# Two units of 768 columns in place of three of 512 for the rest tile of each batch

## The chip, the cores and the metric

One Trainium2 chip, one core. The metric is device time in microseconds (us) of the whole program. Runs agree within about 0.3%.

## The reference, cut to what matters

```python
# x: (4, 12416, 128), inducing: (32, 128); moe weights 128x1536, 128x1536, 1536x128
h = mab(inducing, x)                 # softmax attention, 32 rows a batch
y = mab(x, h)                        # softmax attention back to 12416 rows
out = (relu(y @ w_gate) * (y @ w_val)) @ w_out
```

12416 rows are 97 tiles of 128. The kernel works on pairs of 512-row blocks, eight tiles at once: 12 pairs make 96 tiles and one tile is left, the rest tile.

## The kernel before

The hidden width 1536 is twelve chunks of 128. A full unit is one chunk for a pair, 2 x 512 columns: gates into two PSUM banks (tag `g`, three banks in all), values into a two-bank buffer (tag `v`, two buffers), Relu of the gates on ScalarE, product on VectorE. Because `y @ w` is taken as `p2 @ (h @ w)`, a matmul contracts over only 32 rows, and matmuls on the four row groups of the array can overlap.

A rest unit is four chunks of one tile, 4 x 128 columns, all in one gate bank and one row group:

```python
for s in range(3):
    yield dict(
        mm=[[(slice(i * P, (i + 1) * P), 4 * s + i, p2[r : r + 32, 0:P], hgv[r : r + 32, :])
             for i in range(4)]
            for r in (0, 64)],              # r = 0: gates, r = 64: values
        dst=gvr[:, 4 * s : 4 * s + 4, :].rearrange("p i c -> p (i c)"))
```

The main loop walks in slots, one new unit in each. Here is its order (cut; a "fill" is a piece of other work):

```python
values()                       # TensorE: values of the unit of two slots ago
for m in unit["mm"][0]: gate(*m)   # TensorE: gates of the new unit
for f in post.pop(at, []): f()     # ScalarE etc.: copies of the slot before
# ... 1 to 3 steps of the output chain (o_ps, one bank), and at most one "fill"
nc.scalar.activation(..., func=AF.Relu)       # gates of the new unit
nc.vector.tensor_tensor(..., op=ALU.mult)     # product of the unit of two slots ago
```

A fill is a piece of other work. Three of them, near the end of each of the first three batches, are the pieces of `h @ w` for the next batch: four matmuls into a gate bank, and a 512-column copy on ScalarE one slot later.

```python
for k in range(3):
    ev_hgv(b, k, at + 2, at + 9 + 3 * k)      # earliest and latest slot
```

"The border" below is the passage from the last full units of a batch through its rest units to the first full units that follow.

The softmax here doesn't subtract the row's maximum and nothing guards it: scores larger than these inputs give would overflow.

Of the kernel before, what the change touches and what calls it, by code (L numbers as in the profile page):

```python
# [12 lines left out]
AF = mybir.ActivationFunctionType  # L13
# [5 lines left out]
def kernel(  # L19
# [20 lines left out]
    P = 128  # L40
# [23 lines left out]
    def st(shape, dtype, tag, bufs, name=None):  # L64
        return sb.tile(shape, dtype, tag=tag, bufs=bufs, name=name or tag)
# [273 lines left out]
    count = itertools.count()  # L339


    SPB = NPAIR * NFF + 3


    def slot(b, pr, s):
        if b == B - 1 and pr >= NPAIR - 1:
            return b * SPB + (NPAIR - 1) * NFF + (3 if pr < NPAIR else 0) + s
        return b * SPB + pr * NFF + s

    def order(b):  # L350
# [304 lines left out]
    def chain(w, gv, key, k, t0, first):  # L655
        c = {}
        nt = w // P

        def step(i):
            if i == 0:  # L660
                c["ps"] = bank("o", "o_ps")
            nc.tensor.matmul(  # L662
                c["ps"][:, 0:w], wo[:, i, :], gv(i), start=(i == 0), stop=(i == NFF - 1)
            )

        def evac(at):
            oT = st([P, BLK], FP16, "oT", 4)
            nc.scalar.copy(out=oT[:, 0:w], in_=c["ps"][:, 0:w])  # L668

            def tr():  # L670
                o16 = st([P, TPB, P], FP16, "o16", 4)
                nc.sync.dma_start_transpose(out=o16[:, 0:nt, :], in_=oT[:, 0:w])

                def scale():
                    osb = st([P, TPB, P], FP32, "osb", 4)
                    z = z2is[key + (k,)]
                    for t in range(nt):
                        zz = z[:, t, :]
                        nc.gpsimd.tensor_scalar(  # L679
                            out=osb[:, t, :],  # L680
                            in0=o16[:, t, :],
                            scalar1=zz,
                            scalar2=zz,
                            op0=ALU.mult,
                            op1=ALU.mult,
                        )

                    def store():
                        nc.sync.dma_start(
                            out=ov[key[0]][:, t0 : t0 + nt, :], in_=osb[:, 0:nt, :]  # L690
                        )

                    post[at + 8].append(store)

                post[at + 5].append(scale)

            post[at + 1].append(tr)

        if w == BLK:
            steps = [(first if i == 0 else 0, lambda i=i: step(i)) for i in range(NFF)]  # L700
            counts = (6, 5)
            if key[0] == B - 1 and key[1] == NPAIR - 2:
                counts = (6, 5) if k == 0 else (4, 4)
        else:
            steps = [(first + i // 4, lambda i=i: step(i)) for i in range(NFF)]
            counts = ([4, 8], [4, 8])
        job(steps, evac, counts)

# [69 lines left out]
    def units():  # L778
        for b in range(B):
            for pr in order(b):  # L780
                base = slot(b, pr, 0)
                p2, hgv = p2s.get((b, pr)), state[b]["hgv"]
                if (b, pr) == (B - 1, NPAIR - 1):
                    gvs = [st([P, 6, 2, BLK], FP16, "gv", 4) for _ in range(2)]
                    for k in range(2):
                        steps, evac = last_block(
                            lambda i, g=gvs[k]: g[:, i // 2, i % 2, :],
                            (b, pr),
                            k,
                            (2 * pr + k) * TPB,  # L790
                            k == 1,
                            lambda i, k=k: base + 3 + 6 * k + i // 2,
                        )
                        job(steps, evac, ([1, 3, 3, 3, 3] if k == 0 else [5] * 8,) * 2)
                    for u in range(NFF):
                        k = u // 6
                        p2 = p2s[(b, pr, k)]
                        yield dict(
                            mm=[
                                [  # L800
                                    (
                                        slice(d * BLK, (d + 1) * BLK),
                                        2 * (u % 6) + d,
                                        p2[r : r + 32, :],
                                        hgv[r : r + 32, :],
                                    )
                                    for d, r in ((0, 64 * j), (1, 64 * j + 32))
                                ]
                                for j in range(2)
                            ],  # L810
                            dst=gvs[k][:, u % 6, :, :].rearrange("p k c -> p (k c)"),
                            parts=2 if u == NFF - 1 else 1,
                        )
                elif pr < NPAIR:
                    gvs = []

                    def gv(i, k, gvs=gvs):
                        return gvs[i // 6][:, i % 6, k, :]

                    for k in range(2):  # L820
                        chain(
                            BLK,
                            lambda i, k=k, gv=gv: gv(i, k),
                            (b, pr),
                            k,
                            (2 * pr + k) * TPB,
                            base + 10 + 6 * k,
                        )
                    for s in range(NFF):
                        if s % 6 == 0:  # L830
                            gvs.append(st([P, 6, 2, BLK], FP16, "gv", 4))
                        yield dict(
                            mm=[
                                [
                                    (
                                        slice(k * BLK, (k + 1) * BLK),
                                        s,
                                        p2[r : r + 32, :],
                                        hgv[r : r + 32, :],
                                    )  # L840
                                    for k, r in ((0, 64 * j), (1, 64 * j + 32))
                                ]
                                for j in range(2)
                            ],
                            dst=gvs[-1][:, s % 6, :, :].rearrange("p k c -> p (k c)"),
                            parts=2 if base + s == 0 else 1,
                        )
                else:
                    gvr = st([P, NFF, P], FP16, "gvr", 1)
                    chain(P, lambda i, g=gvr: g[:, i, :], (b, pr), 0, NT - 1, base + 4)  # L850
                    for s in range(3):
                        yield dict(
                            mm=[
                                [
                                    (
                                        slice(i * P, (i + 1) * P),
                                        4 * s + i,
                                        p2[r : r + 32, 0:P],
                                        hgv[r : r + 32, :],
                                    )  # L860
                                    for i in range(4)
                                ]
                                for r in (0, 64)
                            ],
                            dst=gvr[:, 4 * s : 4 * s + 4, :].rearrange("p i c -> p (i c)"),
                        )

    def form(ps, cols, s, p2, hgv):
# [1 line left out]

    def gate_banks(unit):

        n = unit["dst"].shape[-1] // BLK
        unit["g"] = [None] * n

        def gate(cols, s, p2, hgv):
            k, lo = divmod(cols.start, BLK)
# [19 lines left out]
    while True:  # L897
# [64 lines left out]

        if unit:
            g16 = unit["g16"] = st([P, 2 * BLK], FP16, "g16", 4)
            for k, ps in enumerate(unit["g"]):
                nc.scalar.activation(out=g16[:, k * BLK : (k + 1) * BLK], in_=ps, func=AF.Relu)  # L966
        if ready:
            n = ready["dst"].shape[-1]
            w = n // ready.get("parts", 1)
            for a in range(0, n, w):  # L970
                nc.vector.tensor_tensor(  # L971
                    out=ready["dst"][:, a : a + w],
                    in0=ready["g16"][:, a : a + w],
                    in1=ready["v"][:, a : a + w],
                    op=ALU.mult,
                )
        at += 1

# [29 lines left out]
```

## Time and profile before

| what | before |
|---|---|
| time, median of 3 | 708.84 us |
| VectorE, ScalarE, TensorE busy | 96%, 96%, 90% |
| full products (128x1024) | 574, 1213 ns each, 654.9 us busy |
| rest products (128x512) | 12, 685 ns each, 8.0 us busy |
| VectorE idle in the second border of the trace (363.25 to 366.25) | 0.42 + 0.58 us |

VectorE and ScalarE are both nearly full, so the shares do not say which sets the pace. VectorE runs full products without a gap for 50 to 150 us at a time, and at each border it waits about 1 us for TensorE. ScalarE idles there too:

```profile
193.67 0.60 ACT L966 ACTIVATE g<-g_ps 128x512 f16<-128x512 f32 x1 [0.33 <-PE g_ps L869]
194.78 1.09 ACT L966 ACTIVATE g<-g_ps 128x512 f16<-128x512 f32 x2 [0.51 <-PE g_ps L869]
...
196.22 5.04 ACT L966 ACTIVATE g<-g_ps 128x512 f16<-128x512 f32 x10
```

These are ScalarE's lines of the first border: start, length, operation, count, and in brackets the idle time before with what ended it.

### The profile page before, as it was taken

To read this page: it belongs to the slowest core of one execution; us is meant where nothing else is said; L and a number is where in the kernel's file an instruction comes from. 1 tells how busy PE (TensorE), PEld (TensorE's weight loads), DVE (VectorE), ACT (ScalarE), POOL (GpSimd) and SP (SyncE) were. 2 spreads that over 40 slices of the span, in tenths; PEclk is the share of its full clock that TensorE was granted. 3 is DMA by queue.
4 is the path that set the end of the run, shared out by engine and by line. 5 is a ranking of instruction groups with operands and counts; after the bars stand their busy time and mean duration, and the time that the engine had idled before them with its cause. 6 is when DMAs were issued, how large, how long until landed. Compare 5 with 4: busy or idle time off the path is not lost. (4 is left out here: it accounts for less than half of the span.)

```text
span 706.6 us, 14082 instructions
## 1 busy us (share of the span) xinstructions
PE 637.6 (90%) x4629; PEld 186.5 (26%) x4629; DVE 677.7 (96%) x619; ACT 676.1 (96%) x1384; POOL 350.4 (50%) x646
## 2 busy tenths in 40 slices
PE   6899999999988999999998999999999888888997
PEld 5422222222222222222222222222222222222224
DVE  4699999999999999999999999999999999999997
ACT  5799999999999999999999999999999999999996
POOL 3627636544275637356255472753516443534543
PEclk9999999999999999999999999999999999999999
DMA  8656666431258867523149666653223132231222
GB/s 342 219 137 178 161 169 165 109 94 47 84 141 166 201 162 215 118 77 84 53 88 218 169 171 167 165 120 81 63 68 93 50 90 59 78 90 50 71 58 89
DMA packets 142346, 87.58 MB, mean 124 GB/s; under 512 B 117152, under 2 KB 125632, under 8 KB 139968
## 3 DMA queue, kind: packets, MB, share of 16 engines
q1 hardware_dynamic: 142128, 86.62, 46.6%
q8 instruction: 36, 0.59, 0.4%
q14 instruction: 38, 0.31, 0.2%
q10 hardware_dynamic: 144, 0.07, 0.0%
HBM read 27.80 MB, written 25.43 MB: 75 GB/s over the span
## 5 line engine op out<-in xcount | busy, mean ns | idle before, releaser
L971 DVE TENSOR_TENSOR gv<-g,v_ps 128x1024 f16<-128x1024 f16 (+1 forms) x578 | 657.5, 1209 | 9.9 <-PE g_ps L869 6.0
L966 ACT ACTIVATE g<-g_ps 128x512 f16<-128x512 f32 x1164 | 604.2, 618 | 11.9 <-PE g_ps L869 8.4
L662 PE MATMUL o_ps<-gv,wo 128*128 128x512 f16 x1128 | 352.6, 384 | 43.9 <-ACT oT L668 43.9
L679 POOL TENSOR_SCALAR osb<-o,z2i 128x128 f32<-128x128 f16 x380 | 165.9, 452 | 280.5 <-DMA o<-oT 278.6
L869 PE MATMUL g_ps<-p,hgv 32*128 32x512 f16 x1152 | 284.1, 380 | 1.7 <-ACT g L966 1.0
L869 PE MATMUL v_ps<-p,hgv 32*128 32x512 f16 x1152 | 223.6, 383 | 8.7 <-DVE gv L971 6.9
L869 PEld LDWEIGHTS <-hgv 32*128 32x128 f16 x2400 | 69.8, 91 | 267.2 <-issue 263.1
L662 PEld LDWEIGHTS <-wo 128*128 128x128 f16 x1176 | 81.0, 97 | 212.3 <-issue 195.9
L430 POOL TENSOR_TENSOR z2i<-zt,minus 128x16 f32<-128x16 f32 (+3 forms) x31 | 73.2, 2365 | 0.3
L668 ACT CAST oT<-o_ps 128x512 f16<-128x512 f32 (+1 forms) x98 | 58.4, 596 | 0.1
L501 POOL CAST x<-x 128x2048 f16<-128x2048 f32 x18 | 34.0, 1890 | 14.1 <-DMA x<-in_x_dram 13.9
L423 POOL TENSOR_TENSOR zt<-zt 128x32 f32<-128x32 f32 (+5 forms) x124 | 35.1, 283 | 9.7
L423 POOL TENSOR_TENSOR zt<-p2T 128x256 f32<-128x256 f16 (+3 forms) x31 | 17.4, 562 | 24.3 <-DMA p2T<-p 14.0
L270 DVE COPY xT<-xT_ps 128x1024 f16<-128x1024 f16 (+1 forms) x13 | 8.4, 650 | 9.8 <-PE xT_ps L269 8.9
L269 PE MATMUL xT_ps<-eye,x 128*128 128x128 f16 x97 | 9.0, 242 | 5.2 <-POOL x L281 4.6
L282 ACT CAST x<-gv 128x512 f16<-128x512 f32 (+1 forms) x12 | 7.2, 597 | 6.8 <-DMA gv<-in_x_dram 6.8
L195 ACT ACTIVATE p2q<-s_ps 128x512 f16<-128x512 f32 x22 | 13.4, 611 | 0.0
L281 POOL CAST x<-gv 128x512 f16<-128x512 f32 (+1 forms) x12 | 7.2, 598 | 10.1 <-DMA gv<-in_x_dram 10.0
L532 ACT ACTIVATE p1T<-s1T_ps 128x512 f16<-128x512 f32 x18 | 11.1, 615 | 0.0
L179 PE MATMUL s_ps<-xT,hT 128*32 128x512 f16 x108 | 10.8, 389 | 0.1
L971 DVE TENSOR_TENSOR gvr<-g,v_ps 128x512 f16<-128x512 f16 x12 | 8.0, 685 | 1.7 <-PE g_ps L869 1.7
L606 POOL TENSOR_TENSOR hp<-hp,hq 128x129 f32<-128x129 f32 (+1 forms) x18 | 8.2, 458 | 2.5 <-ACT hq L605 2.5
(92 smaller groups left out, 159.5 us busy)
## 6 DMA issues: line engine op xcount, KB each, us to landing
out_dram<-osb SPq DMA_DIRECT2D x95, 256.0 KB, 2.2
x<-in_x_dram SPq DMA_DIRECT2D x18, 1024.0 KB, 5.6
gv<-in_x_dram SPq DMA_DIRECT2D x11, 512.0 KB, 7.4
p<-p2q SPq DMA_DIRECT2D x88, 64.0 KB, 2.0
o<-oT SPq DMA_TRANSPOSE x98, 2.4
x<-in_moe_w_out_dram SPq DMA_DIRECT2D x1, 768.0 KB, 9.1
gv<-in_x_dram SPq DMA_DIRECT2D x2, 256.0 KB, 10.3
x<-in_moe_w_gate_dram SPq DMA_DIRECT2D x1, 512.0 KB, 8.8
```

The costliest lines, as they stand in the source:

```text
L179: nc.tensor.matmul(ps[32 * r : 32 * r + 32, :], hT[:, 0:M], xTs(xT, blocks[r] * TPB, TPB), start=True, stop=True,)
L195: nc.scalar.activation(out=p2q, in_=ps, func=AF.Exp, scale=sm_scale)
L423: nc.gpsimd.tensor_tensor(out=dst, in0=v[:, :, :, 0:m], in1=v[:, :, :, m : 2 * m], op=ALU.add)
L430: nc.gpsimd.tensor_tensor(out=z2i, in0=v[:, :, :, 0], in1=minus1[:, 0 : n * g].rearrange("p (n g) -> p n g", n=n), op=ALU.pow,)
L501: nc.gpsimd.tensor_copy(out=s["x16"][:, t0:t1, :], in_=s["x32", q])
L532: nc.scalar.activation(out=p1T, in_=ps, func=AF.Exp, scale=sm_scale)
L662: nc.tensor.matmul(c["ps"][:, 0:w], wo[:, i, :], gv(i), start=(i == 0), stop=(i == NFF - 1))
L668: nc.scalar.copy(out=oT[:, 0:w], in_=c["ps"][:, 0:w])
L679: nc.gpsimd.tensor_scalar(out=osb[:, t, :], in0=o16[:, t, :], scalar1=zz, scalar2=zz, op0=ALU.mult, op1=ALU.mult,)
L869: nc.tensor.matmul(ps[:, cols], hgv[:, s * P : (s + 1) * P], p2, start=True, stop=True)
L966: nc.scalar.activation(out=g16[:, k * BLK : (k + 1) * BLK], in_=ps, func=AF.Relu)
L971: nc.vector.tensor_tensor(out=ready["dst"][:, a : a + w], in0=ready["g16"][:, a : a + w], in1=ready["v"][:, a : a + w], op=ALU.mult,)
```

## The change

The intent: save one slot in each batch. Three chunks go to either gate bank, so a rest unit holds six chunks in two banks, its matmuls use both row groups, and two units do the rest tile.

```diff
-    SPB = NPAIR * NFF + 3
+    SPB = NPAIR * NFF + 2
...
-            steps = [(first + i // 4, lambda i=i: step(i)) for i in range(NFF)]
+            steps = [(first + i // 6, lambda i=i: step(i)) for i in range(NFF)]
...
-                    for s in range(3):
+                    for s in range(2):
                         yield dict(
                             mm=[
                                 [
                                     (
-                                        slice(i * P, (i + 1) * P),
-                                        4 * s + i,
+                                        slice(k * BLK + i * P, k * BLK + (i + 1) * P),
+                                        6 * s + 3 * k + i,
                                         p2[r : r + 32, 0:P],
                                         hgv[r : r + 32, :],
                                     )
-                                    for i in range(4)
+                                    for i in range(3)
+                                    for k, r in ((0, 64 * j), (1, 64 * j + 32))
                                 ]
-                                for r in (0, 64)
+                                for j in range(2)
                             ],
...
+            w = unit["dst"].shape[-1] // 2
             for k, ps in enumerate(unit["g"]):
-                nc.scalar.activation(out=g16[:, k * BLK : (k + 1) * BLK], in_=ps, func=AF.Relu)
+                nc.scalar.activation(
+                    out=g16[:, k * w : (k + 1) * w], in_=ps[:, 0:w], func=AF.Relu
+                )
...
+            for a in range(parts2):
+                ks = slice(a, a + 1) if parts2 == 2 else slice(0, 2)
                 nc.vector.tensor_tensor(
-                    ...
+                    out=dst[:, ks, :], in0=g16[:, ks, :], in1=v[:, ks, 0:w], op=ALU.mult
                 )
```

More of the change, by code (lines that the diff above doesn't have):

```diff
@@ L339 @@
     count = itertools.count()
-    SPB = NPAIR * NFF + 3
+    SPB = NPAIR * NFF + 2
     def slot(b, pr, s):
         if b == B - 1 and pr >= NPAIR - 1:
-            return b * SPB + (NPAIR - 1) * NFF + (3 if pr < NPAIR else 0) + s
+            return b * SPB + (NPAIR - 1) * NFF + (2 if pr < NPAIR else 0) + s
         return b * SPB + pr * NFF + s
@@ L860, in units @@
                                     )
-                                    for i in range(4)
+                                    for i in range(3)
+                                    for k, r in ((0, 64 * j), (1, 64 * j + 32))
                                 ]
-                                for r in (0, 64)
+                                for j in range(2)
                             ],
-                            dst=gvr[:, 4 * s : 4 * s + 4, :].rearrange("p i c -> p (i c)"),
+                            dst=gvr[:, 6 * s : 6 * s + 6, :].rearrange("p i c -> p (i c)"),
                         )
@@ L871, in gate_banks @@
     def gate_banks(unit):
-        n = unit["dst"].shape[-1] // BLK
-        unit["g"] = [None] * n
+        unit["g"] = [None] * 2
         def gate(cols, s, p2, hgv):
@@ L964 @@
             g16 = unit["g16"] = st([P, 2 * BLK], FP16, "g16", 4)
+            w = unit["dst"].shape[-1] // 2
             for k, ps in enumerate(unit["g"]):
-                nc.scalar.activation(out=g16[:, k * BLK : (k + 1) * BLK], in_=ps, func=AF.Relu)
+                nc.scalar.activation(
+                    out=g16[:, k * w : (k + 1) * w], in_=ps[:, 0:w], func=AF.Relu
+                )
         if ready:
-            n = ready["dst"].shape[-1]
-            w = n // ready.get("parts", 1)
-            for a in range(0, n, w):
+            w = ready["dst"].shape[-1] // 2
+            parts2 = ready.get("parts", 1)
+            dst, g16, v = (
+                t.rearrange("p (k c) -> p k c", k=2)
+                for t in (ready["dst"], ready["g16"][:, 0 : 2 * w], ready["v"])
+            )
+            for a in range(parts2):
+                ks = slice(a, a + 1) if parts2 == 2 else slice(0, 2)
                 nc.vector.tensor_tensor(
-                    out=ready["dst"][:, a : a + w],
-                    in0=ready["g16"][:, a : a + w],
-                    in1=ready["v"][:, a : a + w],
-                    op=ALU.mult,
+                    out=dst[:, ks, :], in0=g16[:, ks, :], in1=v[:, ks, 0:w], op=ALU.mult
                 )
```

## The prediction

> **What bounds the kernel now.** I read the page's busy shares first, then the groups of instructions kept apart by form, then the timelines of the engines around one batch border (the third batch ends the same way 169.06 us after the second).
>
> The busy shares:
>
> ```profile
> PE 637.6 (90%) x4629; PEld 186.5 (26%) x4629; DVE 677.7 (96%) x619; ACT 676.1 (96%) x1384; POOL 350.4 (50%) x646
> ```
>
> VectorE and ScalarE look equally full. The groups by form show what fills them (count, busy us, mean ns, idle before):
>
> ```profile
> L971 DVE TENSOR_TENSOR gv<-g,v_ps 128x1024 f16<-128x1024 f16 x574 | 654.9, 1213 | 8.6 <-PE g_ps L869 6.0 <-ACT p1T L532 0.7 <-ACT hgv L170 0.7
> L966 ACT ACTIVATE g<-g_ps 128x512 f16<-128x512 f32 x1164 | 604.2, 618 | 11.9 <-PE g_ps L869 8.4 <-PE v_ps L869 0.7
> ...
> L971 DVE TENSOR_TENSOR gvr<-g,v_ps 128x512 f16<-128x512 f16 x12 | 8.0, 685 | 1.7 <-PE g_ps L869 1.7
> ```
>
> 574 full products are nearly the whole of VectorE's time, and the rest tile only 8.0 us. Now the border, VectorE (start, length, count, idle before):
>
> ```profile
> 188.53 5.74 DVE L971 TENSOR_TENSOR gv<-g,v_ps 128x1024 f16<-128x1024 f16 x5 [0.78 <-PE g_ps L869]
> 194.20 1.31 DVE L971 TENSOR_TENSOR gvr<-g,v_ps 128x512 f16<-128x512 f16 x2
> 195.92 0.69 DVE L971 TENSOR_TENSOR gvr<-g,v_ps 128x512 f16<-128x512 f16 x1 [0.41 <-PE g_ps L869]
> 197.19 9.22 DVE L971 TENSOR_TENSOR gv<-g,v_ps 128x1024 f16<-128x1024 f16 x8 [0.58 <-PE g_ps L869]
> ```
>
> In long stretches VectorE never rests: 132 full products take 149.75 us (a stretch from 535.12), so one costs (149.75 - 1.21) / 131 = 1.134 us, the part of its 1.213 that does not lie under its neighbour. ScalarE keeps such a pace with room: its ten Relus from 196.22 take 5.04 us, (5.04 - 0.60) / 9 = 0.49 us each, 0.98 a unit. So VectorE sets the pace of a full unit. At the border it idles 0.41 + 0.58 = 0.99 us, waiting for TensorE. Why TensorE is late there:
>
> ```profile
> 193.54 0.82 PE L662 MATMUL o_ps<-gv,wo 128*128 128x512 f16 x3
> 194.33 0.21 PE L869 MATMUL v_ps<-p2r,hgv 32*128 32x128 f16 x1
> 194.34 0.39 PE L869 MATMUL g_ps<-p,hgv 32*128 32x512 f16 x2
> 194.38 0.32 PE L869 MATMUL v_ps<-p2r,hgv 32*128 32x128 f16 x3
> 194.67 0.82 PE L662 MATMUL o_ps<-gv,wo 128*128 128x512 f16 x3
> 195.42 0.23 PE L869 MATMUL v_ps<-p2r,hgv 32*128 32x128 f16 x1
> 195.43 0.39 PE L869 MATMUL g_ps<-p,hgv 32*128 32x512 f16 x2
> 195.49 0.33 PE L869 MATMUL v_ps<-p2r,hgv 32*128 32x128 f16 x3
> 196.39 0.38 PE L662 MATMUL o_ps<-gv,wo 128*128 128x512 f16 x1 [0.57 <-ACT oT L668]
> 196.70 0.39 PE L869 MATMUL v_ps<-p,hgv 32*128 32x512 f16 x2
> ```
>
> The program walks in slots. A slot holds the values of the unit of two slots ago, the gates of a new one, and two or three 512-column steps of the output chain of an earlier pair, whose count hangs on the slot and not on the unit. So a slot with a rest unit in it lasts TensorE as long as one with a full unit: 1.13 us (193.20 to 194.33), 1.09, and 1.28 with the wait for the chain's single bank. VectorE needs only 0.62 us for a rest product (second of the two: 1.31 - 0.69). Three slots carry work for less than two, and that is what the idle time is.
>
> **What the Trainium skill says.** (1) "VectorE: DVE Perf Modes", section "The TRN2 errata", gives (N+151)/0.96 ns for an fp32 tensor_tensor, one column a cycle. The trace agrees: 685 ns at 512, 1213 at 1024, slope 1.03 ns a column. The last product of the kernel (osb, line 740, 384 columns in three blocks with broadcast scales) takes 557 ns, just (384+151)/0.96, so a pattern of several blocks shows no surcharge. (2) "ScalarE: Activation LUTs", section "What ACT_TABLE_LOAD costs": an ACTIVATE with immediates takes 186 ns + 0.833 per column, neighbours overlapping by about 93. That is 613 at 512 (trace: 618), and about 506 at 384, an estimate. The trace's overlap is larger, 0.618 - 0.49 = 0.127. (3) "PSUM — Partial Sum Buffer", section "PSUM bank collisions raise a hardware error": different row tiles may not write one bank at once. This explains the old form (one bank, four matmuls behind each other in one row group) and why the new one can use both row groups: each has its own bank. The trace shows row groups overlapping: g_ps and v_ps start within 0.01 us of each other.
>
> **The change part by part**, for one border (there are four).
>
> VectorE: three products of 512 become two of 768. With the slope 1.0 ns a column, from (1.134 - 0.62) / 512, a 768 product costs 0.62 + 0.26 = 0.88 us. 3 x 0.62 = 1.86 becomes 1.76: -0.10 us. One instruction's fixed part disappears.
>
> ScalarE: three Relus of 512 become four of 384. 0.49 - 128 x 0.833 ns = 0.385; 4 x 0.385 = 1.54 against 1.47: +0.07 us, on an engine that idles 0.33 + 0.51 us here (before 193.67 and 194.78, for TensorE's gates). It hides.
>
> TensorE: 24 matmuls of 128 columns either way. In a slot they run beside the other operand's, which takes 0.33 us to the first chain step in every slot seen, so nothing gained or lost but the alternating row groups (at most 0.05 us).
>
> The slot: each batch has 146 instead of 147. This is the real item. Replay it with the numbers above, TensorE's slot starts kept (193.20, 194.33, 195.42), each now carrying the next unit. First rest product at 194.20 as now; second at 195.08 (values done by 194.70); first full product of the next batch at 195.96, since its values, started at 195.42, take 0.39 and the product follows 0.10 later (as 196.70 to 197.19 shows), 195.91. Now it starts at 197.19. The next slot still waits for the chain's bank: ScalarE's copy of the chain comes after one more Relu pair, at about 195.85 instead of 195.75, so that slot begins at about 196.80 instead of 196.70, its values are usable at 197.29, and the second full product starts there after an idle of 0.2. Before: 197.19 + 1.13 = 198.33. Gain 1.04 us. From here TensorE needs 0.98 us a plain slot (197.74, 198.72, 199.70) against 1.134 and keeps up, but closely: the rest tile's own chain and the next pair's then stand in adjacent slots, where now one slot in between has no chain step. I take 0.05 to 0.15 off for that: about 0.95 to 1.0 for each of three borders.
>
> The last border is different. Pair 11 follows the rest tile there, and in its first slots TensorE runs three and four chain steps, so it paces (687.30, 688.55, 689.85, 691.15). The last products end earlier by one slot, but the final chain (48 matmuls of 128, about 62 ns each, 1.29 us for 20 of them from 699.20) keeps its slots. Now its second part waits for the last values (700.42 to 700.75) and 0.20 for VectorE; without them it ends near 699.20 + 48 x 0.062 + 0.2 = 702.4 instead of 703.0. Gain 0.6.
>
> Sum: 3 x 0.98 + 0.6 = 3.5 us. 708.84 - 3.5 = 705.3.
>
> **Rivals.** (a) TensorE takes all of it back: the same chain work now lies in one slot fewer, and the 45.7 us that TensorE waits for the chain's bank (94 times) grow. Then only VectorE's 0.1 a batch is left: 708.4. For it: TensorE is 90% busy and is the releaser at this border. Against: plain slots leave 0.15 us each, and VectorE runs 49 products without a gap after the border. (b) Gate banks: a rest unit now takes two of the three instead of one, so TensorE cannot run ahead, and ScalarE has the four Relus: 709 to 710. Against: full units take two each and ScalarE leads. (c) The product is now written in two blocks for every full unit as well. If a block cost 10 ns, 574 x 10 ns = 5.7 us would eat the gain: 711. Against: the 557 ns of line 740. (d) The whole slot is saved at all four borders, 1.25 + each: 703.9.
>
> **Range and chances.** The replay carries the middle, 705.3; (d) bounds it below, a half-taken (a) above. 8 in 10: 704.2 to 707.2. Two per cent is 14 us, more than all idle time of VectorE between 28 and 700 us; so within 2%: 0.98, 0.01 for either side.
>
> **What would show it.** Right: 8 products of 128x768 near 945 ns (768+140 cycles); 16 Relus of 384 near 510 ns; the full products unchanged at 1213; at each border no idle before the first full product and 0.1 to 0.3 before the second; the second batch's border 1 us, the third 2 us earlier. Wrong: full products over 1218 ns (c); new idle of VectorE some 8 to 12 products after the border, where the chains are now adjacent (a); ScalarE or TensorE waiting for gate banks in the rest slots (b); a total above 707.2.

## More of the kernel before

The fourth border (the last batch) has no fill for the next batch: there is no next batch. There the rest tile comes before the last pair, and the kernel ends with two special chains of 48 small matmuls each.

## The result, and the profile after

The changed kernel took 706.18 us (median of 4, 706.00 to 706.47) against 708.68 (median of 4) for the kernel before in the same rounds: 2.5 us less. The ratio is 0.9963 (95% interval 0.9946 to 0.9981). A ratio here is the mean time of one kernel's fast runs over the mean of the other's in the same rounds, so not quite the ratio of the medians. By the 2% rule the two are the same; the interval lies below 1.

The groups by form of the changed kernel (count, busy us, mean ns, idle before):

```profile
L980 DVE TENSOR_TENSOR gv<-g,v_ps 128x1024 f16<-128x1024 f16 x574 | 655.5, 1216 | 7.4 <-PE g_ps L871 4.2 <-ACT p1T L532 0.7 <-ACT hgv L170 0.7
...
L980 DVE TENSOR_TENSOR gvr<-g,v_ps 128x768 f16<-128x768 f16 x8 | 7.4, 950 | 0.0
L968 ACT ACTIVATE g<-g_ps 128x384 f16<-128x384 f32 x16 | 7.0, 491 | 0.3
```

The instruction costs are as worked out: 950 ns for 945 predicted, 491 for 510, and the full products, now written as two blocks, 1216 for 1213. Those 3 ns (times 574, 1.7 us) are not what is missing: from full product 0 to 130, where VectorE sets the pace, the two traces keep step within 0.02 us.

VectorE at the first border after the change:

```profile
188.91 5.88 DVE L980 TENSOR_TENSOR gv<-g,v_ps 128x1024 f16<-128x1024 f16 x5 [0.78 <-PE g_ps L871]
194.71 1.86 DVE L980 TENSOR_TENSOR gvr<-g,v_ps 128x768 f16<-128x768 f16 x2
196.75 11.64 DVE L980 TENSOR_TENSOR gv<-g,v_ps 128x1024 f16<-128x1024 f16 x10 [0.17 <-PE g_ps L871]
```

The 0.99 us of idle time have become 0.17 visible (the views print gaps from 0.15 us on; the last row goes on past the end of this view, 208). But to compare, the start of this run has to be taken out. The first of the five products ahead of the border starts at 188.91 here and 188.53 before: 0.38 late, and the lateness is from the loading phase at the very start (VectorE's longest wait there, at 18 to 19 us, is 2.02 us in place of 1.56). This start differs from run to run; in two of the runs below, a stretch of half clock falls into it. The first full product of the next batch starts at 196.75 - 0.38 = 196.37 on the old scale, where it stood at 197.19 and was predicted at 195.96: a gain of 0.82 in place of 1.23.

All 574 full products can be put side by side in this way. Starts in us, from the two traces:

| full product, counted from 0 | before | changed | difference |
|---|---|---|---|
| 138, ahead of border 1 | 188.53 | 188.91 | +0.38 |
| 150, after it | 205.19 | 204.91 | -0.28 |
| 282, ahead of border 2 | 357.28 | 357.14 | -0.14 |
| 294, after it | 374.26 | 373.49 | -0.77 |
| 426, ahead of border 3 | 526.16 | 525.56 | -0.60 |
| 438, after it | 543.13 | 541.90 | -1.23 |
| 558, ahead of border 4 | 679.14 | 677.71 | -1.43 |
| 564, after it | 689.05 | 686.38 | -2.67 |
| the last scaling of the output (VectorE) | 703.05 | 700.66 | -2.39 |
| end of the span | 706.6 | 704.6 | -2.0 |

So the borders gave 0.66, 0.63, 0.63 and 1.24 us, where 0.98 (three times) and 0.6 were forecast. Between borders 1 and 4 small amounts came and went (+0.14, +0.17, -0.20). After border 4, 0.28 were given back by the final chain and 0.4 by the last store. (Where a step below is given from two traces, it is worked out in this way.)

Why did three borders give half of what the fourth gave? TensorE of the changed kernel at border 1:

```profile
191.77 0.39 PE L871 MATMUL v_ps<-p,hgv 32*128 32x512 f16 x2
191.79 0.81 PE L871 MATMUL g_ps<-p2r,hgv 32*128 32x128 f16 x6
192.54 0.60 PE L662 MATMUL o_ps<-gv,wo 128*128 128x512 f16 x2
193.07 0.39 PE L871 MATMUL v_ps<-p,hgv 32*128 32x512 f16 x2
193.08 0.40 PE L871 MATMUL g_ps<-p2r,hgv 32*128 32x128 f16 x6
```

The six gate matmuls of the first rest unit took 0.81 us, those of the second 0.40. In the trace, the first matmul of the six starts at 191.792 and the next, which writes the other bank, at 192.282. Between the two, at 191.576 + 0.654 = 192.230, ScalarE ends the second Relu of the full unit before. That unit's two banks and the fill's one are the three there are, so the second rest bank is the one that Relu reads. Before the change a rest unit needed one bank and did not wait, and at border 4 of the changed kernel, without a fill, the six took 0.46 (first the kernel before at border 1, then the changed kernel at border 4):

```profile
191.41 0.38 PE L869 MATMUL g_ps<-p2r,hgv 32*128 32x128 f16 x4
```

```profile
680.43 0.46 PE L871 MATMUL g_ps<-p2r,hgv 32*128 32x128 f16 x6
```

ScalarE there:

```profile
192.60 4.09 ACT L968 ACTIVATE g<-g_ps 128x384 f16<-128x384 f32 x8
196.58 0.59 ACT L668 CAST oT<-o_ps 128x512 f16<-128x512 f32 x1
197.05 5.04 ACT L968 ACTIVATE g<-g_ps 128x512 f16<-128x512 f32 x10
```

No bracket is left, here or in the lines ahead: the visible idle time of 0.33 and 0.51 us is gone, and ScalarE goes on without one until 245.53 (a gap of 0.14 us before 195.61 is just too short to be printed). The chain's copy starts at 196.58 - 0.38 = 196.20 on the old scale, 0.45 later than before and 0.35 later than I had replayed.

### The profile page after: what moved, and what is told of

Same layout as the page of the kernel before. It is cut to its first block, busy times and chain, and to the rows that moved or that the text cites. A ratio compares the mean times of both kernels' runs of the same rounds, so it can differ in the third digit from the quotient of the medians.

```text
span 704.6 us, 14074 instructions
## 1 busy us (share of the span) xinstructions
PE 635.6 (90%) x4629; PEld 184.6 (26%) x4629; DVE 677.5 (96%) x615; ACT 676.4 (96%) x1388; POOL 348.8 (50%) x646
## 4 chain that ended last, share of the span: by engine, by line
PE 32%; ACT 32%; issue 17%; DVE 13%; DMA 4%; SPq 1%; POOL 1%; ACTq 0%; POOLq 0%; DVEq 0%
ACT g L968 23%; PE o_ps L662 15%; DVE gv L980 13%; PE v_ps L871 10%; ACT oT L668 5%; PE g_ps L871 5%; DMA gv<-in_x_dram 2%; ACT p2q L195 2%; ACT p1T L532 1%; PE h_ps L584 1%; DMA p2T<-p2q 1%; DVE gvr L980 0%; SPq L507 0%; DMA out_dram<-osb 0%; PE idle_ps L263 0%
## 5 line engine op out<-in xcount | busy, mean ns | idle before, releaser
L968 ACT ACTIVATE g<-g_ps 128x512 f16<-128x512 f32 (+1 forms) x1168 | 604.6, 616 | 8.8 <-PE g_ps L871 4.4
L871 PEld LDWEIGHTS <-hgv 32*128 32x128 f16 x2400 | 68.2, 91 | 267.1 <-issue 263.3
L269 PEld LDWEIGHTS <-x 128*128 128x128 f16 x97 | 6.5, 108 | 6.7 <-POOL x L281 6.0
```

The source lines that it names most:

```text
L269: nc.tensor.transpose(ps[:, t - t0, :], x16[:, t, :], eye16)
L871: nc.tensor.matmul(ps[:, cols], hgv[:, s * P : (s + 1) * P], p2, start=True, stop=True)
L968: nc.scalar.activation(out=g16[:, k * w : (k + 1) * w], in_=ps[:, 0:w], func=AF.Relu)
```

## The experiments

My theory after the result: the gain is the slot; the fill in front of the border takes part of it back, because ScalarE and the gate banks no longer have slack there. Rivals: the gain is the shape of the units; the loss comes from the bank alone; ScalarE has room and TensorE or VectorE limits. Differences between traces are given with the start taken out (each run's shift at full product 100).

**1. The shape without the slot.** The changed kernel with an empty third slot after the rest units.

```diff
-    SPB = NPAIR * NFF + 2        # and the same 2 in slot()
+    SPB = NPAIR * NFF + 3
...
+                    yield None   # after the two rest units
```

> The changed kernel with a third, empty slot after the two rest units of each batch, so that it has 147 slots a batch again: the shape of the units without the slot saved. If the gain is the slot (my theory), it goes: 708.2 to 709.2 us, within 0.6 us of the kernel before. If the gain is the shape (two products and two row groups in place of three products), it stays: 705.8 to 706.8.

Measured: 709.46 us, ratio 1.0008 (0.9996 to 1.0021). The gain is gone, so it was the slot. The measured time even lies a little above my range. VectorE at border 1:

```profile
194.41 1.81 DVE L981 TENSOR_TENSOR gvr<-g,v_ps 128x768 f16<-128x768 f16 x2
197.53 9.22 DVE L981 TENSOR_TENSOR gv<-g,v_ps 128x1024 f16<-128x1024 f16 x8 [1.30 <-ACT g L969]
```

VectorE now idles 1.30 us in one piece. In the traces borders 1 to 3 are 0.26, 0.29 and 0.29 us slower than before, border 4 exactly as before (0.00). So the new shape costs 0.26 to 0.29 us at the three borders with a fill and nothing at the one without, and the slot saved is worth the difference between the two runs: 0.66 + 0.26 = 0.92 at border 1, 0.92 at the others, 1.24 at the fourth.

**2. The second bank without the slot.** Three rest units as before, but each spread over two banks, and so with six Relus of 256 columns in place of three of 512.

```diff
-                    for s in range(2):            # and 3 slots, i // 4
+                    for s in range(3):
-                                        6 * s + 3 * k + i,
+                                        4 * s + 2 * k + i,
-                                    for i in range(3)
+                                    for i in range(2)
```

> The kernel before with its three rest units of 512 columns spread over two gate banks (256 columns in each, two Relus a unit): the cost of the second bank alone, no slot saved. If a second bank makes the first rest gates wait for ScalarE (seen as 0.44 us in the changed kernel) and six Relus of 256 cost 0.2 us more than three of 512, it is slower than before: 709.2 to 710.4. If the bank costs nothing where VectorE idles anyway: 708.4 to 709.0.

Measured: 709.00 us, ratio 1.0005 (0.9991 to 1.0019), at the edge between the two expectations. The trace decides what the time cannot: the first rest unit's gates now wait,

```profile
191.66 0.76 PE L871 MATMUL g_ps<-p2r,hgv 32*128 32x128 f16 x4
...
192.90 0.29 PE L871 MATMUL g_ps<-p2r,hgv 32*128 32x128 f16 x4
```

0.76 us against 0.29 for the second unit's. Borders 1 to 3 become 0.17, 0.20 and 0.21 us slower, border 4 stays. So the second bank brings the wait, but with three slots most of it still hides; how much of the 0.2 us is the bank and how much the longer Relus, this run does not separate. Another 0.43 us, at one product of the fourth batch (number 441), is no effect of the edit: the clock granted from 544.86 us on was 0.5 for 3.41 us, and the two value matmuls of a slot took 0.61 us there in place of 0.39. That profiled run took 709.68 us; the three runs with a clock of 0.999 or 1.0 took 708.94 to 709.00.

**3 and 4. The fill after the border.**

```diff
-                    ev_hgv(b, k, at + 2, at + 9 + 3 * k)
+                    ev_hgv(b, k, at + 2 if k < 2 else at + 20, at + 9 + 3 * k if k < 2 else at + 20)
                     # and at + 22 in the second of the two
```

> The changed kernel with the third piece of the next batch's h x weights product moved from the slot ahead of the first rest unit to five slots later (the third slot of the next batch). That piece takes a gate bank and a ScalarE copy. Theory: the first rest gates no longer wait 0.44 us for a bank, so each of three borders gains up to 0.3 more: 705.0 to 705.7. Rival: ScalarE paces the whole border, and the copy only moves: 705.9 to 706.5, with the wait again after the piece's new place.

> The same with the piece two slots further on. Theory: as the run before, 705.0 to 705.7. Rival (ScalarE paces): 705.9 to 706.5. If the two placings differ by more than 0.3 us, the place decides and not the bank alone.

Measured: 706.50 us (ratio 0.9969, 0.9957 to 0.9982) and 706.66 (0.9971, 0.9959 to 0.9984). Neither gained: my theory missed, the rival's range just holds the first, and the second lies above both. But the traces show more. The later of the two, VectorE:

```profile
194.30 1.81 DVE L980 TENSOR_TENSOR gvr<-g,v_ps 128x768 f16<-128x768 f16 x2
196.03 5.98 DVE L980 TENSOR_TENSOR gv<-g,v_ps 128x1024 f16<-128x1024 f16 x5
202.42 4.75 DVE L980 TENSOR_TENSOR gv<-g,v_ps 128x1024 f16<-128x1024 f16 x4 [0.41 <-PE g_ps L871]
```

The border without the fill has no idle bracket. Its first full product starts 1.26 us earlier than before, its second 1.12 earlier: the two numbers of the replay in the prediction, 1.23 and 1.04. The six gates of the first rest unit take 0.46 us there, as at border 4, in place of 0.81. Then, just where the fill now stands, VectorE idles 0.41 and the gain shrinks to 0.48 (to 0.64 with the other placing, so the place counts as well). TensorE shows the same wait as at the border, now in a full unit:

```profile
198.60 0.39 PE L160 MATMUL hgv_ps<-wv,hT 128*32 128x512 f16 x2
198.93 0.39 PE L871 MATMUL v_ps<-p,hgv 32*128 32x512 f16 x2
198.95 0.86 PE L871 MATMUL g_ps<-p,hgv 32*128 32x512 f16 x2
```

**5 and 6. The fill ahead of the border**, alone and with the repair of run 7.

```diff
-                    ev_hgv(b, k, at + 2, at + 9 + 3 * k)
+                    ev_hgv(b, k, at + 2 if k < 2 else at + 8, at + 9 + 3 * k if k < 2 else at + 8)
```

> The changed kernel with the same third piece moved seven slots earlier, into a slot of the pair before the rest units where TensorE waits for the chain's bank anyway. The two later placings showed the border itself gain 1.12 us without the piece and give 0.5 to 0.6 back where it landed. If a slot of the pair has room for it, the border keeps about 1.1 us: three times 0.45 better than the changed kernel, 704.8 to 705.3. If ScalarE has no room there either, 0.4 to 0.6 us come back ahead of the border and the time stays at 705.9 to 706.5.

> The same together with the rest tile's chain of the last batch in one slot (which gave 0.4 us by itself). If the piece finds room: 704.4 to 704.9, the fastest of all; if not: 705.5 to 706.0.

Measured: 706.29 us (ratio 0.9965, 0.9952 to 0.9977) and 706.56 (0.9965, 0.9951 to 0.9978). The better cases did not come.

```profile
183.53 4.85 DVE L980 TENSOR_TENSOR gv<-g,v_ps 128x1024 f16<-128x1024 f16 x4 [0.21 <-PE g_ps L871]
...
194.82 1.81 DVE L980 TENSOR_TENSOR gvr<-g,v_ps 128x768 f16<-128x768 f16 x2
196.55 2.49 DVE L980 TENSOR_TENSOR gv<-g,v_ps 128x1024 f16<-128x1024 f16 x2
```

VectorE's new idle of 0.21 us stands at 183.53, where the piece went. From the traces the piece cost 0.48 us there (0.29, 0.06 and 0.13 at three products), and the border then gained 1.13: 0.65 net, as in the changed kernel. So the piece costs about half a microsecond at three of the four places tried and 0.64 at the later placing of run 4. That the old border, with its own idle time, had held it for free is not shown by a run that moves it there; run 11 below, where an added Relu cost that border nothing, speaks for it. The second kernel's median lies above its range. Three of its five runs have a clock of 0.996 or 0.997 and take 706.56 to 706.76, the two at 1.0 take 706.08 and 706.12; in the profiled one the clock was 0.5 for 3.41 us from 20.63 on, and the start was 0.92 us later than that of the kernel before. With the start out, its span is 2.73 us shorter than before, near run 7's 2.78.

**7. The end of the kernel.** In the last batch the rest tile's chain takes one slot instead of two, so both final chains start a slot earlier.

```diff
-            counts = ([4, 8], [4, 8])
+            counts = ([4, 8], [4, 8]) if key[0] < B - 1 else ([12], [12])
```

> The changed kernel with the rest tile's output chain of the last batch done in one slot instead of two, so that the two final chains start one slot earlier against the last pair's units, as they stood before the change. If the final chain being one slot late costs time (the step of my prediction that took 0.4 us off at the last border), this gives 705.4 to 705.9. If TensorE is the bound in the whole tail, its work is only reordered: 706.0 to 706.5.

Measured: 705.82 us (705.61 to 706.02), ratio 0.9959 (0.9947 to 0.9972): within the first range. With the start out, the last scaling comes 0.29 us earlier than in the changed kernel (3.06 against 2.77 before the old time), and the span is 0.46 shorter. The final chain that this edit moves, in TensorE's lines of the kernel before and of the changed kernel:

```profile
699.20 1.29 PE L727 MATMUL o_ps<-wo,gv 128*128 128x128 f16 x20
700.42 0.39 PE L869 MATMUL v_ps<-p,hgv 32*128 32x512 f16 x2
700.75 1.68 PE L727 MATMUL o_ps<-wo,gv 128*128 128x128 f16 x24
702.62 0.40 PE L727 MATMUL o_ps<-wo,gv 128*128 128x128 f16 x4 [0.20 <-DVE gv L971]
```

```profile
697.77 2.85 PE L727 MATMUL o_ps<-wo,gv 128*128 128x128 f16 x48
```

Before, the chain was broken by the last values and at the end waited for VectorE. After, it runs in one piece of 48 behind everything else: VectorE's last product ends about 1 us before it, and TensorE sets the end. The output's last scaling follows at 700.66.

**8 and 9. The last store.** The stores of the last batch two slots earlier, alone and with run 7's repair; the changed kernel once more beside them.

```diff
-                    post[at + 8].append(store)
+                    post[at + (8 if key[0] < B - 1 else 6)].append(store)
```

> The changed kernel once more, on the chip of the two runs below: 706.0 to 706.5 us. Its first product of all starts anywhere from 26.8 to 28.0 us (the input's arrival), which is noise of the start and not of the borders.

> The changed kernel with the stores of the last batch issued two slots earlier, so that the rest tile's store no longer stands 0.87 us ahead of the last store of all. If the last store's longer landing (3.35 us after the change against 2.93 before) comes from that neighbour, 0.2 to 0.4 us come back: 705.7 to 706.1. If not: the same as the changed kernel.

> Both repairs of the end together: the rest tile's chain of the last batch in one slot, and its stores two slots earlier. If the two are separate terms (0.4 us of TensorE's final chain, 0.3 of the last store): 705.3 to 705.7, faster than both kernels. If the chain's repair already contains the store's: 705.7 to 706.0.

Measured: the changed kernel again 706.31 us (ratio 0.9970, 0.9958 to 0.9983); stores earlier 706.08 (0.9965, 0.9953 to 0.9978); both repairs 705.71 (0.9961, 0.9948 to 0.9975).

By the medians the second of these lies within my range and the third just inside the second of its two, but the trace does not bear the reason out. In the changed kernel as repeated, the last three stores are issued at 700.37, 700.76 (the rest tile's) and 701.61 us; with the earlier stores the middle one is gone, the others stand at 700.47 and 701.70. Yet the span still ends 705.0 - 701.70 = 3.3 us after the last issue, against 705.0 - 701.61 = 3.4. So it was not that neighbour. What does go with the landing is the distance from the other store, of the last pair's first block: 1.74 us ahead in the kernel before (landing 2.9), 1.41 in run 7 (3.2), 1.26 in the changed kernel (3.35). That is a pattern in these runs and not a test. Runs 7 and 9 do not differ beyond their spread; I take run 7's edit as the version to keep. It is faster than the kernel before by 0.4% (the same by the 2% rule), and its slowest run (706.02) is about as fast as the fastest of the changed kernel (706.00 and 706.11 in its two sets).

**10 and 11. More work for ScalarE at the border**, in both kernels: one Relu of 512 columns into a tile that nobody reads, at borders 1 to 3.

```diff
+    def more_act(b):
+        junk = st([P, BLK], FP16, "junk", 2)
+        nc.scalar.activation(out=junk, in_=state[b]["hgv"][:, 0:BLK], func=AF.Relu)
+
+    for b in range(B - 1):
+        post[slot(b, NPAIR, 0) + 1].append(lambda b=b: more_act(b))
```

> The changed kernel with one more ScalarE instruction (a Relu of 512 columns into a tile nobody reads, 0.49 us) in the second rest slot of each of the first three batches. If ScalarE paces the border now, each costs most of its length: plus 0.8 to 1.5 us, 707.0 to 707.7. If VectorE or TensorE paces it and ScalarE has room, as I predicted: no more than 0.3 slower.

> The kernel before with the same extra ScalarE instruction in the same slot. ScalarE idles 0.33 and 0.51 us there, so if that idle time is real room it swallows most of it: 708.6 to 709.2. If ScalarE paces the border before the change too: 709.5 to 710.2.

Measured: in the changed kernel 708.16 us (707.03 to 708.20, ratio 0.9987, 0.9974 to 0.9999), in the kernel before 708.57 (ratio 1.0003, 0.9989 to 1.0017). The first lies above both of my ranges. Of its 2 us over the changed kernel, half is no effect of the edit: in its profiled run the clock was 0.5 for 3.41 us from 17.77 on and the first product of all started at 27.99 us instead of 27.16, and the two of its five runs with a clock of 0.999 were 1.1 us faster (707.03 and 707.11, inside the first range) than the three at 0.997 and 0.998. With the start out, each of the three borders lost 0.31 us, nearly 0.95 in all. In the kernel before the same three instructions cost 0.00, 0.00 and 0.00. VectorE and ScalarE of the changed kernel with the extra instruction:

```profile
195.54 0.95 DVE L987 TENSOR_TENSOR gvr<-g,v_ps 128x768 f16<-128x768 f16 x1
196.77 0.95 DVE L987 TENSOR_TENSOR gvr<-g,v_ps 128x768 f16<-128x768 f16 x1 [0.28 <-PE g_ps L871]
```

```profile
194.19 0.63 ACT L896 ACTIVATE junk<-hgv 128x512 f16<-128x512 f16 x1
194.71 1.86 ACT L975 ACTIVATE g<-g_ps 128x384 f16<-128x384 f32 x4
```

The bracket blames TensorE, but the instruction that was added is ScalarE's: TensorE waited for the banks that ScalarE empties (the two gates of the next full unit start 0.46 us apart, at 194.80 and 195.26, and 0.15 apart in the changed kernel). This is the test of "ScalarE has room here": before the change it had room for the whole 0.49 us, and after it for no more than 0.18.

## Why the prediction was right or wrong

The time, 706.18 us, lies in the range of 704.2 to 707.2, and within 2% was right. The gain was 2.5 us where 3.5 were forecast. By its steps:

- **What bounds the kernel, and that the slot is the real item:** right. The empty slot gave the whole gain back. With the fill moved away the border made the replay's two numbers (1.26 and 1.12 us for 1.23 and 1.04).
- **VectorE, two products of 768:** right (950 ns for 945). Rival (c), a surcharge for the two-block form on all full products, fell: 1216 ns against 1213.
- **ScalarE, "It hides":** this step failed. The added 0.07 us is about right by itself, but the room of 0.84 us that I took for free was what the shorter border uses up, and the third piece's copy stands in it. In the terms of the sum, a border of the first three gave 0.63 to 0.66 us in place of 0.98: 0.92 for the slot, less 0.26 to 0.29 for the new shape, which had been put at nothing. (The 0.92 is worked out from the other two numbers.) The two runs with the extra Relu show the missing room directly, 0.31 us each against 0.00.
- **Rival (b), gate banks:** dismissed with "full units take two each and ScalarE leads". It was half right: the wait is there (0.81 us for six gates, 0.46 with the fill moved away), but what goes with it is the missing third of a border and not the whole gain. What the argument missed is that a fill takes a bank too, and that the old one-bank unit could follow a fill without waiting (0.38 us for four gates). How much of the piece's half microsecond is bank, TensorE time or ScalarE time is not separated by these runs.
- **"TensorE needs 0.98 us a plain slot":** misread. In the old trace a slot of the same work took 0.87 us (191.39 to 192.26). 0.98 is two Relus of 0.49, ScalarE's pace, seen through TensorE's banks (in those slots the two gates take 0.50 us in place of 0.39). It was in my own numbers, and would have pointed to ScalarE as the limit after the border.
- **The last border, 0.6:** the sum is near, 0.52 with the start out (a gain of 2.32 in the span, less 1.80 before border 4), but by two errors that cancel. The chain of 48 matmuls took 2.85 us: (2.85 - 0.22) / 47 = 56 ns each, and not 62, and the 0.20 us of waiting for VectorE went. The lines that I read give 56 as well when the length of the last matmul, 0.22 us, is taken off, (1.29 - 0.22) / 19. So does the Trainium skill, "VectorE: DVE Perf Modes", section "The TRN2 errata": max(60, 6 + columns) cycles at 2.4 GHz for a matmul, 56 ns at 128 columns; I had not used it. And the last store landed 0.4 us later, which I had not looked at. That the final chain stands a slot late and so costs some tenths is confirmed by run 7 (0.29).
- **Rival (a), new idle time 8 to 12 products after the border:** not borne out. Product 150, the eighth after the border, waits 0.07 us, where the kernel before waited 0.06 at the one ahead of it, and TensorE's waits for the chain's bank grew only from 45.7 to 46.5 us in all.
- **Not foreseen:** small shifts inside the batches (+0.14, +0.17, -0.20). They also came with the empty slot and not with the three two-bank units, so they hang on two units a batch instead of three and not on the slot or on the two-block form. The buffers of `v` (two) and `g16` (four) then fall differently; that this is the way it works is a guess, and stays open.
- **A slip of reading:** the 169.06 us in the prediction's first lines lie between the first border and the second (197.19 and 366.25); the third came 168.87 after the second. Nothing rests on it.

## What to carry to other kernels

A slot saved at a border where engines idle is worth what the engine chain needs there, and not the idle time of the bound engine: ask who else was using that idle time, here a copy on ScalarE and a third bank, which then cost about half a microsecond at each of the four places tried. Widening a unit into a second buffer of a ring that also serves other work turns an unnoticed neighbour into a wait; look at what stands in the ring one slot earlier. To read gains of a few tenths of a microsecond, line up the same instruction in two traces, take the noise of the start out, and look at the clock of each trace for stretches of half clock. Over one border the differences repeat to a few hundredths (0.65, 0.61, 0.62 and 1.24 us when the changed kernel was traced again), where the medians move by 0.3. Over the whole run they do not: with the start out, the two traces of the changed kernel still end 0.36 us apart, most of it in steps of at most 0.03 us at a product.

## What the Trainium skill lacked or had wrong

- "ScalarE: Activation LUTs", section "What ACT_TABLE_LOAD costs": neighbours overlap by about 93 ns there; here 618 ns instructions followed each other every 0.49 us, an overlap of about 127. Relus of 384 columns took 491 ns, where its formula gives 506 (an estimate), and the pair started 0.387 us apart (192.605 and 192.992).
- None of the pages cited gives the size of the cost that decided here: with one gate matmul waiting for a bank (0.49 us between the first and the second of six), the chain steps and the values behind it came late too, by 0.44 and 0.43 us with the start out (192.54 and 193.07 against 191.72 and 192.26).
